# Convolution and maxout FFN on one core: who adds the two k1 halves, how PSUM tiles take turns, and where three buffers lie

## The chip, the cores and the metric

The kernel runs on one core of a Trainium2 chip. The metric is device time in microseconds, the median of several runs. TensorE (PE) multiplies matrices into PSUM; VectorE (DVE), ScalarE (ACT) and GpSimd (POOL) do the arithmetic around it; SyncE (SP), ACT and POOL issue the DMAs. In the rows of the profile PE is a matmul, PEld a weight load, and "q" behind an engine's name its sequencer or DMA queue. Line numbers are those of the kernel before; behind the diff's additions the same lines of the changed kernel stand one to some twenty further down.

## The reference

Four sequences of 12544 positions with 128 channels (`x`, `v`) go through a long convolution and then through a feed-forward block:

```python
h_filt = (np.maximum(pos_emb @ w1, 0) @ w2) * exp(-0.01 * pos)     # filter, 128 channels
u = x * v
y = irfft(rfft(u, 2S) * rfft(h_filt, 2S))[:S]                      # causal convolution along the sequence
x2 = (x * y).reshape(50176, 128)
h = np.maximum(np.maximum(x2 @ m1, x2 @ m2), x2 @ m3)              # 128 -> 768
out = h @ w_out                                                    # 768 -> 128
```

All is in float32. The kernel writes the maximum as `x2 @ m1` plus a maximum of relu and a difference: `max(relu(x2 @ (m2 - m1)), x2 @ (m3 - m1))`. The part with m1 goes through a product of m1 and w_out, `lin`, that is made once. So one hidden block of 128 costs two matmul groups, pa and pb, and one down projection.

## The kernel before, in words

**Stages.** A prologue (to about 320 us) converts weights, transforms the filter into the table hd in DRAM, and does the whole convolution of sequence 0 up to its last transform. Then come three passes of the main loop: the FFN of sequence b (0, 1, 2) runs on PE, and beside it, in small steps, the convolution of sequence b + 1. A last stage (from about 1913 us) does the FFN of sequence 3 with fewer products, sums of hidden blocks on POOL taking their place.

**The main loop.** Sequence b has 32 tiles (NT) of 4 x 98 positions, and each has six hidden blocks f (NF). One f of one tile is a slot; a pass has 192. In each slot `up` (L697) makes pa = 128x392 in PSUM (two halves of 64 columns, L154), relu into hid by ACT (L701), then pb, and DVE takes the maximum of hid and pb (L704). `down` (L710), two slots later, adds hid times w_out into ops; at the tile's end ACT copies ops to ot (L717) and POOL issues the store (L719).

**The last transform of the convolution.** For each tile, `t_load` fetches zt, two arrays z0 and z1 of 90x512 (two values of k1), and xT, through SP's queue. `t_sums` (L665) turns them into their sum (even, L669) and difference (zt, L670). In the later half of sequences 1 to 3 a sign is needed, and DVE does both with scalar_tensor_tensor (L673); elsewhere the engine is the caller's choice: POOL, and DVE for a sequence's first tile. They are called for the next tile at f = 0 (f = 3 in a sequence's last tile). `t_last` (L677) multiplies them by the table f4p into yps, at f = 3, 4 or 2, and DVE multiplies yps by xT into gt (L691), the FFN's input. The table f4p and a column of signs are loaded once, at the head of the main loop, through ACT's queue.

**The convolution beside it.** `conv_steps` (L575) plans it in slots. First the 32 units of the sequence are loaded, multiplied, transposed by DMA and put through the first transform (`u_first`, ps1, L408, DVE L419 into spec). When all are there, from slot s0 (55 for sequence 1, 62 for 2 and 3) on, 45 pairs g follow. A pair is: psq = middle transforms by matmul (`g_quarter`, L462 for pair g, L472 for the way back of pair z = g - 3), a fold (`g_fold`, ACT L484, DVE L487 twice into cb), swaps on ACT (`q_swap`), two multiplications by the filter ht on DVE (L506, L511), the add of the two on POOL (L514), and two unfolds on DVE (L518, cb to xs), which L472 needs three pairs on. POOL stores z to DRAM (`g_store`, L495).

The planner holds a table `load` of costs per slot. Folds have fixed slots; each multiplication and unfold is put into the emptiest slot of its allowed few. A slot in which DVE sums costs 1.4 more.

**Order.** [...] A matmul's bank is set when the program is built: a pool with n buffers gives out the one whose use ended first in the builder's order. The hps pool has three banks for pa and pb; cps has two double banks for ps1, psq and yps (three single ones in the last stage).

**Buffers.** hp holds zt, xT, even, gt and hid; op_ holds ot; op_ and the convolution's pools are released before the last stage, whose pool lp is laid over them. The last stage's relu results are in lp, and before its second block DVE makes five differences of parts of w_out and lin (L1090).

Of the kernel before, what the change touches and what calls it, by code (L numbers as in the profile page):

```python
# [1 line left out]

# [22 lines left out]
N1 = 90  # L25
NH = 82
HH = NH // 2
LATE = 3
# [61 lines left out]
def kernel(  # L90
# [15 lines left out]
    nc = tc.nc  # L106
    NG, _, _, B, NB = x.shape
# [3 lines left out]
    NF = DFF // P  # L111
    NK = N1 // 2
# [286 lines left out]
    def u_first(u, i0=0, n=4):  # L399


        t = uts[u] if i0 + n < 4 else uts.pop(u)
        ps = cps.tile([P, 256 * n], FP32, tag="cv", name="ps1")
        at = 4 * u + i0
        for i in range(n):
            for h in range(2):
                for c in range(2):
                    nc.tensor.matmul(  # L408
                        ps[64 * c:64 * c + 64, 256 * i + h * N1:256 * i + (h + 1) * N1],
                        t[:, 2 * ((at + i) % 8) + h].rearrange("n r t -> n (r t)"),  # L410
                        f1q[:, h, c * N1:(c + 1) * N1],
                        start=(i % 2 == 0 and h == 0), stop=True, skip_group_check=True)
        v = ps[:].rearrange("p (s m) -> p s m", m=256)[:, :, 0:2 * N1].rearrange(
            "p s (h k) -> p h k s", h=2)
# [37 lines left out]
    def g_quarter(g, z):  # L452


        ps = cps.tile([P, 1024], FP32, tag="cv", name="psq")
        if g is not None:
            w, t = ws.pop((g, 0)), sqs.pop(g)
            for k in range(2):
                for r in range(2):
                    for a in range(2):  # L460
                        at = 512 * r + k * D
                        nc.tensor.matmul(  # L462
                            ps[64 * a:64 * a + 64, at:at + D], w[64 * r:64 * r + 64, k, a, :],
                            t[64 * r:64 * r + 64, k, a, :], start=(k == 0), stop=True,
                            skip_group_check=True)
        if z is not None:
            w, ab = ws.pop((z, 1)), abs_.pop(z)
            for q in range(2):
                for a in range(2):
                    for k in range(2):  # L470
                        at = 512 * a + 256 + q * D
                        nc.tensor.matmul(  # L472
                            ps[64 * k:64 * k + 64, at:at + D], w[64 * a:64 * a + 64, k, q, :],
                            ab[64 * a:64 * a + 64, q, k, :], start=(g is None and q == 0),
                            stop=True, skip_group_check=True)
        pss[g, z] = ps
# [95 lines left out]
    def conv_steps(b, done):  # L572


        out = []  # L575
# [17 lines left out]
        def start(x):  # L593
            return s0 + int(x // 2 * 2 * per_pair)

        load = [(1.2 if i % NF == 3 else 0.6) + (1.4 if i % NF == 0 and b > 1 and i >= NT * NF // 2 else 0)
                for i in range(NT * NF)]
        for x in range(NK + LATE):
            s = start(x)
# [34 lines left out]
        return slots, {start(x) + 1 for x in range(NK + LATE)}  # L634


    N = 4 * NB
# [38 lines left out]

    def t_last(i):  # L677
        zt = zts.pop(i)
        ps = cps.tile([P, state["yps"]], FP32, tag="cv", name="yps")
        own = i[0] == B - 1 and i[1] > 1  # L680
        g = (lp if own else hp).tile([D, 4, NB], FP32, tag="g", name="gt", bufs=4 if own else 3)
        y = ps[:, 0:N].rearrange("d (p n) -> d p n", p=4)
# [12 lines left out]

    def up(i, f, tag="hid", bufs=3):
        rhs = gs[i][:].rearrange("d p n -> d (p n)")  # L697
        h = (lp if tag[0] == "h" and tag != "hid" else hp).tile([P, N], FP32, tag=tag, name="hid", bufs=bufs)
        pa = hps.tile([P, 512], FP32, tag="hps", name="pa")
        halves_mm(pa[:, 0:N], w_sb[1][:, f * P:(f + 1) * P], rhs, True, True)  # L700
        nc.scalar.activation(h[:], pa[:, 0:N], Relu)  # L701
        pb = hps.tile([P, 512], FP32, tag="hps", name="pb")
        halves_mm(pb[:, 0:N], w_sb[2][:, f * P:(f + 1) * P], rhs, True, True)
        nc.vector.tensor_tensor(out=h[:], in0=h[:], in1=pb[:, 0:N], op=ALU.max)  # L704
        return h
# [201 lines left out]
    state = {"cv": (cvp, cps), "turn": cps, "xb": 2}  # L907
    pl = sps.tile([D, 512], FP32, name="pl")
    Gs, minus = {}, {}

# [115 lines left out]
    hh = conv.enter_context(tc.tile_pool(name="hh", bufs=2))  # L1026
    cvp = conv.enter_context(tc.tile_pool(name="cvp", bufs=3))
    hps = ctx.enter_context(tc.tile_pool(name="hps", bufs=3, space=PSUM))
    cps = conv.enter_context(tc.tile_pool(name="cps", bufs=2, space=PSUM))
    ops = conv.enter_context(tc.tile_pool(name="ops", bufs=1, space=PSUM))  # L1030
    state = {"yps": 1024}


    tiles = [(b, i) for b in range(B) for i in range(NT)]
# [1 line left out]
    late = []  # L1036
    for n, (b, i) in enumerate(tiles[:LAST]):
        if i == 0:
            beside, folds = conv_steps(b + 1, EARLY if b == 0 else 0)
        if n == 0:  # L1040
            t_load(*tiles[0])
            t_load(*tiles[1])
# [2 lines left out]
        for f in range(NF):  # L1045
# [29 lines left out]


    lp = ctx.enter_context(tc.tile_pool(name="lp", bufs=1))
    cps = ctx.enter_context(tc.tile_pool(name="cps2", bufs=3, space=PSUM))
    state["yps"] = 512
# [83 lines left out]
```

## Time and profile before

| | |
|---|---|
| median of 3 runs | 2338.91 us (2336.47 to 2343.64) |
| profiled execution | 2339.31 us, span 2337.5 us |
| mean granted PE clock | 0.996 |
| busy: PE, DVE, ACT, POOL | 2284.1, 1553.8, 1178.8, 969.0 us |
| L704 DVE maximum | 768, mean 558 ns |
| L701 ACT relu | 768, mean 499 ns |
| L518 DVE unfold | 270, mean 662 ns |
| L514 POOL add | 135, mean 1306 ns |
| L669, L670 on POOL | 61 each, mean 1304 and 1302 ns |
| L669, L670 on DVE | 19 each, mean 1041 and 942 ns |
| L673 on DVE, even and zt | 48 each, mean 870 and 972 ns |
| zt from issue to landing (384 issues of 90 KB) | median 3.1 us |

The profile is of one execution. A row of a timeline gives start, duration, engine, line, operation and tiles; in brackets is the engine's idle time before it and what ended it. A row "x3" is three instructions merged, with the time from the first start to the last end. A row of waits gives who waited for whom: total us, times, longest. Means of a group hide that one instruction can take much longer than another of the same shape. The end of a matmul is modelled: neighbouring matmuls overlap in the rows, so start-to-start is the time that one takes; a group of four pa matmuls starts 0.66 us after the one before it.

### The profile page before, as it was taken

How to read it: one execution, taken by the hardware profiler on the slowest of the kernel's cores; microseconds unless marked ns; L12 is line 12 of the kernel's file. 1: busy time of each engine (PE TensorE's matmuls, PEld its weight loads, DVE VectorE, ACT ScalarE, POOL GpSimd, SP SyncE). 2: the span in 40 equal slices, each digit the busy share in tenths (PEclk: the TensorE clock that was granted, in tenths of full speed). 3: DMA queues.
4: the chain of work that ended last, by engine and by line, in shares of the span. 5: the costliest groups of instructions: out<-in, count | busy, mean ns of one | idle time of the engine just before them, and what ended most of it. 6: DMA issues, size and time to landing. Idle time of an engine off the chain costs nothing.

```text
span 2337.5 us, 68165 instructions
## 1 busy us (share of the span) xinstructions
PE 2284.1 (98%) x27853; PEld 1371.9 (59%) x27853; DVE 1553.8 (66%) x2798; ACT 1178.8 (50%) x2124; POOL 969.0 (41%) x1153
## 2 busy tenths in 40 slices
PE   8999989999999999999999999999999999999998
PEld 7889856655455445655555546655555546666665
DVE  5678856656777746757888846757888855454443
ACT  2678844456666624446666634446666622222222
POOL 1045424424444424324333324324333326666666
PEclk9999999999999999999999999999999999999999
DMA  7868969989998749979999849969999822222221
GB/s 160 201 202 266 290 158 181 165 180 238 226 238 219 198 104 187 188 141 238 240 248 246 226 113 180 192 144 244 242 241 245 223 80 66 54 54 70 65 55 22
DMA packets 473146, 410.93 MB, mean 176 GB/s; under 512 B 328004, under 2 KB 374231, under 8 KB 472834
## 3 DMA queue, kind: packets, MB, share of 16 engines
q1 hardware_dynamic: 433504, 317.61, 62.2%
q0 software_dynamic: 26400, 75.72, 11.2%
q10 hardware_dynamic: 12930, 13.25, 1.8%
q8 instruction: 219, 3.59, 0.7%
q14 instruction: 93, 0.76, 0.1%
HBM read 262.77 MB, written 84.67 MB: 149 GB/s over the span
## 4 chain that ended last, share of the span: by engine, by line
PE 76%; DMA 11%; DVE 5%; issue 3%; ACT 2%; SPq 1%; POOL 0%; ACTq 0%; DVEq 0%; POOLq 0%
PE pa L154 18%; PE pb L154 17%; PE ops L154 14%; PE ops L764 6%; PE ps L408 5%; DMA ht<-hd 4%; PE yps L154 4%; PE ps L163 3%; PE ps L154 2%; DMA zt<-zd 2%; PE psq L472 2%; DVE xs L518 2%; PE psq L462 2%; DMA sq<-spec 2%; DMA wt<-wq_const 1%
## 5 line engine op out<-in xcount | busy, mean ns | idle before, releaser
L701 ACT ACTIVATE hid<-pa 128x392 f32<-128x392 f32 x768 | 383.5, 499 | 756.5 <-PE pa L154 738.3
L704 DVE TENSOR_TENSOR hid<-hid,pb 128x392 f32<-128x392 f32 x768 | 428.2, 558 | 361.9 <-PE pb L154 351.5
L154 PE MATMUL pb<-gt,w_sb 128*64 128x392 f32 x3072 | 640.3, 495 | 10.2 <-ACT hid L701 10.2
L154 PE MATMUL pa<-gt,w_sb 128*64 128x392 f32 x3072 | 644.8, 497 | 0.7 <-DVE gt L691 0.7
L154 PE MATMUL ops<-hid,wo_sb 128*64 128x392 f32 x2304 | 478.1, 493 | 0.0
L154 PEld LDWEIGHTS pb<-gt,w_sb 128*64 128x64 f32 x3072 | 220.6, 137 | 301.2 <-issue 263.2
L514 POOL TENSOR_TENSOR cb<-cb,xs 128x512 f32<-128x512 f32 x135 | 176.3, 1306 | 455.1 <-DVE xs L511 210.5
L154 PEld LDWEIGHTS ops<-hid,wo_sb 128*64 128x64 f32 x2304 | 167.0, 137 | 212.9 <-issue 212.9
L154 PEld LDWEIGHTS pa<-gt,w_sb 128*64 128x64 f32 x3072 | 200.6, 137 | 147.6 <-issue 124.4
L419 DVE TENSOR_TENSOR spec<-ps,high 128x360 f32<-128x360 f32 (+1 forms) x204 | 142.1, 739 | 131.2 <-ACT high L417 130.8
L487 DVE TENSOR_TENSOR cb<-psq,eo 128x512 f32<-128x512 f32 (+1 forms) x288 | 175.3, 650 | 75.1 <-ACT eo L484 74.6
L719 POOL DMA_DIRECT2D out_dram<-ot x96 | 75.3, 785 | 322.2 <-ACT ot L717 293.7
L502 ACT ACTIVATE xs<-cb 32x512 f32<-32x512 f32 x270 | 169.9, 629 | 22.2 <-DVE cb L487 13.4
L518 DVE TENSOR_TENSOR xs<-cb 128x256 f32<-128x256 f32 x270 | 167.5, 662 | 9.8 <-POOL cb L514 9.8
L503 ACT COPY xs<-cb 32x512 f32<-32x512 f32 x270 | 166.7, 617 | 3.2
L417 ACT COPY high<-ps 128x360 f32<-128x360 f32 (+1 forms) x102 | 77.2, 761 | 157.2 <-PE ps L408 126.3
L408 PEld LDWEIGHTS ps<-f1q,uT 98*64 98x64 f32 x3072 | 131.8, 137 | 35.2 <-issue 32.9
L154 PEld LDWEIGHTS yps<-f4p,even 90*64 90x64 f32 x2048 | 116.1, 139 | 40.9 <-issue 35.0
L408 PE MATMUL ps<-f1q,uT 98*64 98x90 f32 x3072 | 136.4, 241 | 3.2 <-DVE spec L419 2.6
L691 DVE TENSOR_TENSOR gt<-yps,xT 128x392 f32<-128x392 f32 x128 | 72.3, 565 | 91.7 <-PE yps L154 52.6
L154 PE MATMUL yps<-f4p,even 90*64 90x49 f32 x2048 | 125.7, 221 | 3.0 <-DMA f4p<-f4p_const 3.0
L154 PE MATMUL yps<-f4p,zt 90*64 90x49 f32 x2048 | 127.3, 223 | 0.0
(130 smaller groups left out, 3306.7 us busy)
## 6 DMA issues: line engine op xcount, KB each, us to landing
ht<-hd SPq DMA_DIRECT2D x264, 256.0 KB, 6.7
wt<-wq_const SPq DMA_DIRECT2D x144, 256.0 KB, 6.4
zd<-cb POOLq DMA_DIRECT2D x135, 256.0 KB, 6.2
zt<-zd SPq DMA_DIRECT2D x384, 90.0 KB, 3.1
sq<-spec SPq DMA_DIRECT2D x264, 128.0 KB, 7.0
ut<-in_xr_dram SPq DMA_DIRECT2D x128, 196.0 KB, 4.3
ut<-in_vr_dram SPq DMA_DIRECT2D x128, 196.0 KB, 4.6
xT<-in_x_dram SPq DMA_DIRECT2D x256, 98.0 KB, 3.6
```

The lines of the kernel that those rows point to most:

```text
L154: nc.tensor.matmul(out[64 * h:64 * h + 64], lhsT[:, 64 * h:64 * h + 64], rhs, start=start, stop=stop, skip_group_check=True)
L408: nc.tensor.matmul(ps[64 * c:64 * c + 64, 256 * i + h * N1:256 * i + (h + 1) * N1], t[:, 2 * ((at + i) % 8) + h].rearrange("n r t -> n (r ...
L417: nc.scalar.copy(high, v[:, 0])
L419: nc.vector.tensor_tensor(out=spec[:, :, a, at:at + n], in0=v[:, 1], in1=high, op=op)
L487: nc.vector.tensor_tensor(out=cb[:, a, lo:hi], in0=ps[:, lo:hi], in1=eo[:, lo:hi], op=op)
L502: nc.scalar.mul(xs[at:at + 32], xt[at + 32:at + 64], -1.0)
L503: nc.scalar.copy(xs[at + 32:at + 64], xt[at:at + 32])
L514: nc.gpsimd.tensor_tensor(out=xts[g], in0=xts[g], in1=xs[:], op=ALU.add)
L518: nc.vector.tensor_tensor(out=ab[:, q], in0=y[:, 0], in1=y[:, 1], op=(ALU.subtract, ALU.add)[q])
L701: nc.scalar.activation(h[:], pa[:, 0:N], Relu)
L704: nc.vector.tensor_tensor(out=h[:], in0=h[:], in1=pb[:, 0:N], op=ALU.max)
L764: nc.tensor.matmul(ps[64 * c:64 * c + 64, 0:H2], w, rhs[:, H2 * c:H2 * c + H2], start=start, stop=True, skip_group_check=True)
```

## The change

1. `t_sums` goes to DVE also for tiles whose slot lies past s0, while pairs run: the sums of tiles 11 to 31 of sequence 0 and of tiles 12 to 15 of sequences 1 and 2. `conv_steps` returns s0 (`pairs_from`), and its `load` counts 1.4 for f = 0 of every tile past s0, not just of the later half.
2. PSUM tiles are made once and taken in turns by `itertools.cycle`: three banks for pa and pb, two double banks for ps1, psq and yps, three single ones for yps in the last stage. In the prologue the pool stays.
3. hid has a pool of its own (hidp), which stays in the last stage; its first three relu results use it. op_ lies with the pools that stay. The five differences are made one at a time after steps 3 to 7 of the last stage instead of all at its start.
4. f4p and the signs are loaded through SP's queue, ahead of the first zt.

```diff
-        ps = cps.tile([P, 256 * n], FP32, tag="cv", name="ps1")
+        ps = state["bank"]()[:, 0:256 * n]
...
-        ps = cps.tile([P, 1024], FP32, tag="cv", name="psq")
+        ps = state["bank"]()
...
-        load = [(1.2 if i % NF == 3 else 0.6) + (1.4 if i % NF == 0 and b > 1 and i >= NT * NF // 2 else 0)
+        load = [(1.2 if i % NF == 3 else 0.6) + (1.4 if i % NF == 0 and i > s0 else 0)
...
-        ps = cps.tile([P, state["yps"]], FP32, tag="cv", name="yps")
+        ps = state["bank"]()
...
-        h = (lp if tag[0] == "h" and tag != "hid" else hp).tile([P, N], FP32, tag=tag, name="hid", bufs=bufs)
-        pa = hps.tile([P, 512], FP32, tag="hps", name="pa")
+        h = (hidp if tag == "hid" else lp).tile([P, N], FP32, tag=tag, name="hid", bufs=bufs)
+        pa = next(hbanks)
...
-        pb = hps.tile([P, 512], FP32, tag="hps", name="pb")
+        pb = next(hbanks)
...
+    hidp = ctx.enter_context(tc.tile_pool(name="hidp", bufs=3))
     hp = ctx.enter_context(tc.tile_pool(name="hp", bufs=3))
+    f4p = hp.tile([N1, 2, 2, NB // 2], FP32, name="f4p", bufs=1)
+    nc.sync.dma_start(f4p[:], f4p_d)
+    sign_t = hp.tile([N1, 1], FP32, name="sign", bufs=1)
+    nc.sync.dma_start(sign_t[:], sign_d)
+    op_ = ctx.enter_context(tc.tile_pool(name="op", bufs=2))
     conv = ExitStack()
-    f4p = hp.tile([N1, 2, 2, NB // 2], FP32, name="f4p", bufs=1)
-    nc.scalar.dma_start(f4p[:], f4p_d)
-    sign_t = hp.tile([N1, 1], FP32, name="sign", bufs=1)
-    nc.scalar.dma_start(sign_t[:], sign_d)
...
-    op_ = conv.enter_context(tc.tile_pool(name="op", bufs=2))
...
+    hbanks = itertools.cycle([hps.tile([P, 512], FP32, name=f"hps{i}") for i in range(3)])
+    pairs = itertools.cycle([cps.tile([P, 1024], FP32, name=f"cps{i}") for i in range(2)])
+    state = {"bank": lambda: next(pairs)}
...
-                t_sums(tiles[n + 1], nc.vector if turn_ else nc.gpsimd)
+                t_sums(tiles[n + 1], nc.vector if turn_ or i * NF > pairs_from else nc.gpsimd)
...
-    for out, a, b in ((tw[:, 1], b22, b12), (b12, b12, b11), (tw[:, 0], b22, b12),
-                      (tw[:, 2], b21, tw[:, 0]), (linx[:], lin[:, 0:64], lin[:, 64:128])):
-        nc.vector.tensor_tensor(out=out, in0=a, in1=b, op=ALU.subtract)
+    weights = [(tw[:, 1], b22, b12), (b12, b12, b11), (tw[:, 0], b22, b12),
+               (tw[:, 2], b21, tw[:, 0]), (linx[:], lin[:, 0:64], lin[:, 64:128])]
...
+            own = (name, BUFS[name]) if step > 2 else ("hid", 3)
             h[name, f] = first if step == 0 else up(
-                (b, i + n), f + (NC if name[2] == "2" else 0), name, BUFS[name])
+                (b, i + n), f + (NC if name[2] == "2" else 0), *own)
+            if step > 2 and weights:
+                out, a1, a2 = weights.pop(0)
+                nc.vector.tensor_tensor(out=out, in0=a1, in1=a2, op=ALU.subtract)
```

More of the change, by code (lines that the diff above doesn't have):

```diff
@@ L1 @@
+import itertools
 from contextlib import ExitStack
@@ L412, in u_first @@
                         start=(i % 2 == 0 and h == 0), stop=True, skip_group_check=True)
-        v = ps[:].rearrange("p (s m) -> p s m", m=256)[:, :, 0:2 * N1].rearrange(
+        v = ps.rearrange("p (s m) -> p s m", m=256)[:, :, 0:2 * N1].rearrange(
             "p s (h k) -> p h k s", h=2)
@@ L633, in conv_steps @@
             slots.setdefault(s, []).append((fn, args))
-        return slots, {start(x) + 1 for x in range(NK + LATE)}
+        return slots, {start(x) + 1 for x in range(NK + LATE)}, s0
     N = 4 * NB
@@ L906 @@
     sps = pro.enter_context(tc.tile_pool(name="sps", bufs=1, space=PSUM))
-    state = {"cv": (cvp, cps), "turn": cps, "xb": 2}
+    state = {"cv": (cvp, cps), "turn": cps, "xb": 2,
+             "bank": lambda: cps.tile([P, 512], FP32, tag="cv", name="ps1")}
     pl = sps.tile([D, 512], FP32, name="pl")
@@ L1027 @@
     cvp = conv.enter_context(tc.tile_pool(name="cvp", bufs=3))
-    hps = ctx.enter_context(tc.tile_pool(name="hps", bufs=3, space=PSUM))
-    cps = conv.enter_context(tc.tile_pool(name="cps", bufs=2, space=PSUM))
+    hps = ctx.enter_context(tc.tile_pool(name="hps", bufs=1, space=PSUM))
+    cps = conv.enter_context(tc.tile_pool(name="cps", bufs=1, space=PSUM))
     ops = conv.enter_context(tc.tile_pool(name="ops", bufs=1, space=PSUM))
-    state = {"yps": 1024}
+    hbanks = itertools.cycle([hps.tile([P, 512], FP32, name=f"hps{i}") for i in range(3)])
+    pairs = itertools.cycle([cps.tile([P, 1024], FP32, name=f"cps{i}") for i in range(2)])
+    state = {"bank": lambda: next(pairs)}
     tiles = [(b, i) for b in range(B) for i in range(NT)]
@@ L1038 @@
         if i == 0:
-            beside, folds = conv_steps(b + 1, EARLY if b == 0 else 0)
+            beside, folds, pairs_from = conv_steps(b + 1, EARLY if b == 0 else 0)
         if n == 0:
@@ L1077 @@
     lp = ctx.enter_context(tc.tile_pool(name="lp", bufs=1))
-    cps = ctx.enter_context(tc.tile_pool(name="cps2", bufs=3, space=PSUM))
-    state["yps"] = 512
+    cps = ctx.enter_context(tc.tile_pool(name="cps2", bufs=1, space=PSUM))
+    singles = itertools.cycle([cps.tile([P, 512], FP32, name=f"last{i}") for i in range(3)])
+    state = {"bank": lambda: next(singles)}
     ops = ctx.enter_context(tc.tile_pool(name="ops2", bufs=1, space=PSUM))
```

## The prediction

> **What bounds the kernel now.** I read the busy shares first, then what TensorE (PE) waits for, then those waits in the timeline.
>
> ```profile
> span 2337.5 us, 68165 instructions
> PE 2284.1 (98%) x27853; PEld 1371.9 (59%) x27853; DVE 1553.8 (66%) x2798; ACT 1178.8 (50%) x2124; POOL 969.0 (41%) x1153
> ```
>
> PE is busy for 2284.1 of 2337.5 us, and the change alters no matmul: the built programs have the same PE order. All it can move is the 53.4 us in which PE stands, and what follows from it. The waits of PE (total, times, longest) over the whole run:
>
> ```profile
> PE pb L154 <- ACT hid L701: 10.2, 12, 3.5
> PE psq L472 <- DVE xs L518: 9.6, 15, 1.0
> PE yps L154 <- DMA f4p<-f4p_const: 3.0, 1, 3.0
> PE psq L472 <- DVE gt L691: 3.0, 1, 3.0
> ```
>
> Nearly all others lie in the opening, which the change leaves alone. The same view for 500 to 830 us alone, where the pairs of sequence 1 run beside the FFN of sequence 0:
>
> ```profile
> PE psq L472 <- DVE xs L518: 4.4, 5, 1.0
> PE psq L472 <- DVE gt L691: 3.0, 1, 3.0
> PE pb L154 <- ACT hid L701: 3.0, 4, 0.9
> ```
>
> Three mechanisms stand behind these rows. **(a)** The PSUM pools give out whichever bank was free first in the build's order. Of 768 pb tiles ten are put where the pa of the same step lies, so PE must wait for that pa's relu. The gaps before pb number exactly ten of 0.59 to 0.91 us, 6.6 us in all (10.2 less the 3.5 of (c) and one of 0.2): 3.0 in this stretch, 3.6 at the starts of sequences 0, 1 and 2. **(b)** psq waits for late L518 results. The timeline shows why (start, us, engine, line):
>
> ```profile
> 630.39 1.27 POOL L514 TENSOR_TENSOR cb<-cb,xs 128x512 f32<-128x512 f32 x1 [5.32 <-ACT hid L701]
> 630.64 4.66 DVE L518 TENSOR_TENSOR xs<-cb 128x256 f32<-128x256 f32 x3
> 632.23 1.37 POOL L669 TENSOR_TENSOR even<-zt 90x512 f32<-90x512 f32 x1
> 633.67 1.34 POOL L670 TENSOR_TENSOR zt<-zt 90x512 f32<-90x512 f32 x1
> ...
> 635.35 0.45 PE L472 MATMUL psq<-xs,wt 64*64 64x128 f32 x8 [0.96 <-DVE xs L518]
> ```
>
> An L518 alone has a median of 419 ns; these three took 4.66 us. One lasted for the add L514 on POOL, one for both sums, L669 and L670. Then psq stands for 0.96 us. Set against POOL's spans, 16 of the 90 L518 here overlap a POOL sum and hold 19.1 us above 419 ns. At 818.19 the same triple (4.64 us) delays gt and gives the 3.0 us wait. **(c)** At the change to the last stage a relu writes memory that output buffers still occupy:
>
> ```profile
> 1912.70 0.76 POOL L719 DMA_DIRECT2D out_dram<-ot  x1 [11.30 <-ACT ot L717]
> 1916.70 0.89 ACT L701 ACTIVATE hid<-pa 128x392 f32<-128x392 f32 x2 [4.31 <-DMA out_dram<-ot]
> 1917.25 1.57 PE L154 MATMUL pb<-gt,w_sb 128*64 128x392 f32 x4 [3.46 <-ACT hid L701]
> 1918.62 1.52 PE L154 MATMUL pa<-gt,w_sb 128*64 128x392 f32 x4
> 1920.93 0.82 PE L154 MATMUL pa<-gt,w_sb 128*64 128x392 f32 x4
> ```
>
> PE stands 3.46 us before pb at 1917.25. After it four pb matmuls last 1.57, and only at 1920.93 0.82 again: three groups take 3.68 us for 1.98, 1.70 us more. After the 3.05 us wait at 820.8 four groups take 4.38 for 2.63, 1.75 more.
>
> [...] 33 L518 beside L514 and the store's issue have a median of 1316 ns for 419, while L704, with one input in PSUM, stays at 557 beside L514. [...]
>
> **The change part by part**, against the profiled execution's 2339.3 us (1.8 of it outside the span; 0.4 above the median of the three).
>
> 1. Strict turns. Every bank is now reused by the third tile on, so the ten waits go: -6.6. But 136 pa tiles used the bank two back, and 136 pb tiles four back; all become three. I set each tile's start in the trace against the end of the reader three tiles earlier: the room is negative only at six pa tiles (1118, 1199, 1295, 1644, 1725, 1821 us), by 0.67 each, because the L704 before is late. That costs 4.0. Within some 5 us after each there is a psq wait of 0.22 to 0.42, 2.1 together, and a PE that starts later finds that L518 done: +1.9 net. For psq and yps the same comparison at two turns gives nothing negative. ACT gets 218 extra semaphore waits before relu; a satisfied one takes 17 ns, and the room of pb behind relu is mostly 1.26 us: 0.
>
> 2. Sums on DVE. 21 tiles of sequence 0 and 4 each of sequences 1 and 2, two instructions each: 58 x 0.68 us (L669 at 325.53, row below). In 500 to 830 DVE gains 42 x 0.68 = 28.7 and loses the 19.1. A moved sum can itself be blocked by L514: in the second halves of sequences 1 and 2, where DVE already sums, 12 of 32 tiles had one that was, by some 0.9; the same share here is 8 of 21, 7 us. So 241.7 becomes some 258 of 330, 78%. Two stretches already run in that state:
>
> ```profile
> 500.00:830.00 330.00, 319.33 (x3572) 164.75 (x3570) 241.69 (x410) 200.51 (x362) 155.62 (x151) 0.99 0.89 218
> 1210.00:1370.00 160.00, 159.55 (x1754) 81.45 (x1750) 126.61 (x223) 96.56 (x176) 50.90 (x54) 1.00 0.85 212
> 1700.00:1872.00 172.00, 171.08 (x1948) 88.48 (x1946) 143.05 (x248) 110.60 (x199) 59.89 (x62) 1.00 0.96 234
> ```
>
> There DVE is at 79% and 83%, and PE stands for 0.45 of 160 and 0.92 of 172 us. That is the best evidence that DVE bears it. Queued behind a sum on DVE are the first L704 of the tile and the pair's arithmetic; for L704 waits pa two steps on. Its room there is mostly 1.78 us, and 0.78 in four tiles (from 565, 582, 696, 713 us): 1.37 - 0.78 = 0.6 x 4 = 2.4. At 820 L518 is blocked by L514 alone, 2.0 shorter: 1.05 remains, too little for the half clock. I leave 0.5 for the first pair. This stretch now loses 10.4 + 1.75 = 12.2 and will lose 4.0: -8.2, of which 3.0 is counted in 1: -5.2. In sequences 1 and 2 the waits of 0.95 at 1068 and 1593, beside POOL sums, go: -1.9. Zt lands 9 us or more before DVE would want it, so no DMA is waited for. The planner moves eight unfolds and two multiplications of the conv of sequence 1, and one unfold each of sequences 2 and 3, by one slot, within the limits that psq's need sets: 0.
>
> 3. Relu buffers, output buffers, table differences. The relu no longer waits for the output's landing: -3.46 - 1.70 = -5.2. The five subtractions (1.7 us) go between L704s; DVE is half idle there (159 of 330 us), and they are needed from step 9: 0.
>
> 4. f4p and sign through SP. Two issues (0.63 and 0.34 us on ACT) stand ahead of zt and xT in SP's queue. f4p no longer lands last, but zt does:
>
> ```profile
> 325.53 0.69 DVE L669 TENSOR_TENSOR even<-zt 90x512 f32<-90x512 f32 x1 [0.30 <-DMA zt<-zd]
> ```
>
> About 1.0 later, the sums end at 327.2 and 327.9, where yps started at 327.11 before. From -0.3 to +1.5; I take +0.6.
>
> Sum: -6.6 + 1.9 - 5.2 - 1.9 - 5.2 + 0.6 = -16.4. 2339.3 - 16.4 = 2322.9; against the median 2338.9, some 2323.
>
> **Rivals.** A: DVE's queue loosens more than I allow, no pa waits, and all psq waits go: 6.6 + 9.6 + 3.05 + 1.75 + 5.2 = 26 saved, 2313. For it: PE's 99.7% at 79% DVE. Against it: the six negative rooms. B: lateness moves from psq to pa, and the stretch keeps its 12.2; sequences 1 and 2 gain nothing. Only 3.6 + 5.2 - 0.6 is won: 2331. For it: strict turns take from pb the four-back room that the build gave just where DVE is late. C, slower: DVE becomes the bound. If L514 blocked a sum in every one of the 29 moved tiles for its whole 1.3 us, the first L704 would come 2.67 later against room 1.78: 0.89 x 25 + 1.89 x 4 = 29.8, less the 2.4 counted: 2350. It decides once the moved tiles lose over 0.8 us each (16.4 + 7 over 29). Against it: 12 of 32. That the change doesn't do what it says is excluded for the order: the build has the 58 sums on DVE and all turns at three and two.
>
> **How the numbers follow.** Mine 0.62, A 0.14, B 0.18, C 0.06. Unknown costs (f4p 2 us, blocked sums some 4, pa waits 2 to 4) spread mine from 2318 to 2330. The range 2315 to 2332 leaves out much of A, part of B and C. This kernel's runs differ by 0.3%, 7 us, and less can't be told from no change; 2331.9 is the border. Faster: nearly all of mine, A, half of B: 0.83; same 0.11; slower 0.06.
>
> **What would show it.** Right: no wait of pb for relu above 0.3 us; no clock dip near 820 and 1915; L518 beside L669 gone; PE standing some 4 us in 500 to 830; pa waiting for DVE hid, about ten times, 0.6 each. Wrong: pa waits for L704 in most moved tiles (C, or B if psq's remain), sums at 1.5 us or more on the mean, or yps waiting past 328 for zt.

## The result, and the profile after

The changed kernel takes 2316.97 us (median of four runs, 2315.53 to 2319.48). The kernel before takes 2339.88 (median of four). The ratio is 0.9903, with a 95% interval of 0.9885 to 0.9921: faster by 1%, some 23 us. The forecast was 2323, with a range of 2315 to 2332.

The busy shares of the changed kernel (columns as before):

```profile
span 2313.7 us, 68365 instructions
PE 2277.5 (98%) x27853; PEld 1379.8 (60%) x27853; DVE 1574.2 (68%) x2856; ACT 1177.5 (51%) x2124; POOL 898.8 (39%) x1095
```

PE is busy for 2277.5 us, not 2284.1, although not one matmul was changed, and it stands for 36.2 us, not 53.4. Of the gain of 23.8 us between the two profiled spans, 17.2 is idle time and 6.6 is "busy" time. The prediction had treated busy time as fixed but for the two stretches at the half clock. This is where it fell short, as shown below.

The waits of PE over the whole run, in the changed kernel. Its PSUM tiles have new names: hps is pa or pb, cps is ps1, psq or yps. Columns are total us, times, longest.

```profile
PE hps L155 <- DVE hid L705: 5.3, 10, 0.9
PE cps L155 <- DVE even L670: 2.8, 1, 2.8
PE cps L473 <- DVE gt L692: 0.5, 1, 0.5
```

The ten pb waits for relu, the fifteen psq waits for xs, the 3.0 us for gt and the 3.5 us at the change to the last stage are gone. In their place stand ten waits of hps (pa) for L705 (the old L704), as the prediction said, and one of 0.5 for gt. The 2.8 us for the first sum takes the place of the 3.0 us for f4p. The same view for 500 to 830 us:

```profile
PE hps L155 <- DVE hid L705: 1.7, 4, 0.4
PE cps L473 <- DVE gt L692: 0.5, 1, 0.5
```

The prediction gave these places 2.4 and 1.05. The load on VectorE there, and in two stretches where it already made the sums before, comes from the view of windows (us, then busy time and instructions of PE, PEld, DVE, ACT, POOL; clock; DMA share; GB/s):

```profile
500.00:830.00 330.00, 327.77 (x3664) 169.60 (x3662) 262.60 (x458) 202.26 (x366) 105.62 (x111) 1.00 0.89 221
1190.00:1350.00 160.00, 159.43 (x1778) 82.08 (x1776) 128.16 (x226) 98.17 (x179) 53.01 (x56) 1.00 0.84 213
1678.00:1850.00 172.00, 170.83 (x1976) 89.16 (x1974) 143.02 (x250) 111.68 (x201) 59.01 (x61) 1.00 0.97 239
```

DVE is busy for 262.6 of 330 us (forecast: some 258), POOL for 105.6 instead of 155.6, and PE stands for 2.2 us instead of 10.7. The triple of L518 that took 4.66 us beside POOL's sums is now L519, and the sums, now on DVE, run after it instead of beside it (timeline of the changed kernel: start, us, engine, line):

```profile
626.83 1.26 POOL L515 TENSOR_TENSOR cb<-cb,xs 128x512 f32<-128x512 f32 x1 [5.42 <-DVE xs L512]
626.97 2.07 DVE L519 TENSOR_TENSOR xs<-cb 128x256 f32<-128x256 f32 x3
628.97 0.68 DVE L670 TENSOR_TENSOR even<-zt 90x512 f32<-90x512 f32 x1
629.12 0.62 PE L473 MATMUL cps<-xs,wt 64*64 64x128 f32 x16
629.68 0.69 DVE L671 TENSOR_TENSOR zt<-zt 90x512 f32<-90x512 f32 x1
```

The triple takes 2.07 us, one of its three still being long beside L515; the sums follow at 0.68 and 0.69, and L473 starts without a wait. At the change to the last stage (timeline):

```profile
1893.48 0.76 POOL L720 DMA_DIRECT2D out_dram<-ot  x1 [11.31 <-DMA zt<-zd]
1894.62 0.50 ACT L702 ACTIVATE hid<-hps 128x392 f32<-128x392 f32 x1 [0.82 <-DVE hid L705]
1892.76 6.42 PE L155 MATMUL hps<-gt,w_sb 128*64 128x392 f32 x38
```

The store is issued at the same point of the work, but the relu after it, which used to wait 4.31 us for its landing, waits for a maximum only, and PE runs through without a gap.

To see where the time comes from I cut the profiled executions at the ends of the maxima (L704, L705 in the changed kernel), counted from one. The column "before" is the length of a stretch in the kernel before; all other numbers are differences to it, in us.

| stretch, by count of L704 | before | forecast | changed | turns alone | sums alone | buffers alone |
|---|---|---|---|---|---|---|
| start to 1 | 333.36 | +0.6 | +0.59 | +0.49 | +2.23 | +0.17 |
| 1 to 60, no pairs | 167.38 | -1.2 | -1.66 | -1.42 | +0.28 | +0.05 |
| 60 to 186, pairs of sequence 1 | 343.03 | -8.2 | -11.18 | -4.24 | -10.84 | -0.02 |
| 192 to 258, no pairs | 190.50 | -1.2 | -1.65 | -1.63 | 0.00 | -0.02 |
| 258 to 384, pairs of sequence 2 | 334.93 | 0 | -1.74 | +0.38 | -1.58 | +1.01 |
| 385 to 571, all of sequence 3 beside the FFN | 512.19 | -1.2 | -3.59 | -0.96 | -0.78 | -0.17 |
| 571 to 591, change to the last stage | 45.43 | -5.2 | -4.54 | +0.29 | -0.47 | -4.54 |
| 591 to the end | 395.26 | 0 | -0.01 | 0.00 | 0.00 | -0.01 |

The stretches left out differ by less than 0.02. Three rows carry noise of up to some 2 us: the start, because the prologue ends at 324.1 us in one execution and at 326.2 in another, and the two rows with the first pairs of sequences 2 and 3, where PE waits by turns for L518 or for a DMA (wt, sq), 0 to 1.5 us in all. The last three columns are the experiments that follow.

### The profile page after: what moved, and what is told of

Same layout as the page of the kernel before. It is cut to its first block, busy times and chain, and to the rows that moved or that the text cites. A ratio compares the mean times of both kernels' runs of the same rounds, so it can differ in the third digit from the quotient of the medians.

```text
span 2313.7 us, 68365 instructions
## 1 busy us (share of the span) xinstructions
PE 2277.5 (98%) x27853; PEld 1379.8 (60%) x27853; DVE 1574.2 (68%) x2856; ACT 1177.5 (51%) x2124; POOL 898.8 (39%) x1095
## 3 DMA queue, kind: packets, MB, share of 16 engines
q0 software_dynamic: 26400, 75.72, 11.2%
q8 instruction: 219, 3.59, 0.7%
## 4 chain that ended last, share of the span: by engine, by line
PE 84%; DMA 6%; ACT 3%; DVE 3%; issue 2%; SPq 1%; ACTq 1%; POOL 0%; DVEq 0%; POOLq 0%
PE hps L155 41%; PE ops L155 17%; PE ops L765 6%; PE cps L409 5%; PE cps L155 4%; PE cps L463 3%; PE ps L164 3%; PE cps L473 2%; DMA ht<-hd 2%; PE last L155 1%; DMA hd<-ht 1%; ACT ht L958 1%; DMA wt<-wq_const 1%; PE pm L324 1%; DMA zt<-zd 1%
## 5 line engine op out<-in xcount | busy, mean ns | idle before, releaser
L155 PE MATMUL hps<-gt,w_sb 128*64 128x392 f32 x6144 | 1150.4, 495 | 6.1 <-DVE hid L705 5.3
L702 ACT ACTIVATE hid<-hps 128x392 f32<-128x392 f32 x768 | 383.9, 500 | 736.6 <-PE hps L155 720.7
L155 PEld LDWEIGHTS hps<-gt,w_sb 128*64 128x64 f32 x6144 | 424.5, 137 | 437.4 <-issue 391.3
L705 DVE TENSOR_TENSOR hid<-hid,hps 128x392 f32<-128x392 f32 x768 | 427.3, 557 | 333.6 <-PE hps L155 323.9
L515 POOL TENSOR_TENSOR cb<-cb,xs 128x512 f32<-128x512 f32 x135 | 181.7, 1346 | 471.4 <-DVE xs L512 331.1
L488 DVE TENSOR_TENSOR cb<-cps,eo 128x512 f32<-128x512 f32 (+1 forms) x288 | 175.1, 649 | 65.6 <-ACT eo L485 65.1
L420 DVE TENSOR_TENSOR spec<-cps,high 128x360 f32<-128x360 f32 x180 | 135.5, 794 | 121.9 <-ACT high L418 121.9
L519 DVE TENSOR_TENSOR xs<-cb 128x256 f32<-128x256 f32 x270 | 141.8, 568 | 7.5 <-POOL cb L515 7.5
L409 PEld LDWEIGHTS cps<-f1q,uT 98*64 98x64 f32 x2880 | 124.9, 137 | 30.6 <-issue 30.6
L409 PE MATMUL cps<-f1q,uT 98*64 98x90 f32 x2880 | 128.1, 241 | 0.4 <-DVE uT L393 0.4
L155 PE MATMUL cps<-f4p,even 90*64 90x49 f32 x1568 | 96.5, 221 | 2.8 <-DVE even L670 2.8
L155 PE MATMUL cps<-f4p,zt 90*64 90x49 f32 x1568 | 97.8, 223 | 0.3 <-DVE zt L671 0.3
```

Of the source, the lines that this page charges most:

```text
L155: nc.tensor.matmul(out[64 * h:64 * h + 64], lhsT[:, 64 * h:64 * h + 64], rhs, start=start, stop=stop, skip_group_check=True)
L409: nc.tensor.matmul(ps[64 * c:64 * c + 64, 256 * i + h * N1:256 * i + (h + 1) * N1], t[:, 2 * ((at + i) % 8) + h].rearrange("n r t -> n (r ...
L488: nc.vector.tensor_tensor(out=cb[:, a, lo:hi], in0=ps[:, lo:hi], in1=eo[:, lo:hi], op=op)
L515: nc.gpsimd.tensor_tensor(out=xts[g], in0=xts[g], in1=xs[:], op=ALU.add)
L519: nc.vector.tensor_tensor(out=ab[:, q], in0=y[:, 0], in1=y[:, 1], op=(ALU.subtract, ALU.add)[q])
```

## The experiments

### The parts one by one

**Strict turns alone.** The kernel before with

```diff
-        pa = hps.tile([P, 512], FP32, tag="hps", name="pa")
+        pa = next(hbanks)
...
-        ps = cps.tile([P, 1024], FP32, tag="cv", name="psq")
+        ps = state["bank"]()
```

(and the same for pb, ps1 and yps). Expected:

> The kernel before with the strict turns alone (part 1); sums, relu and output buffers and the load of f4p as before. My theory: the ten waits of pb for the relu of its own step go (6.6 us in the rows, and some 0.17 more for each, 1.7, because a matmul behind a wait shows no overlap with the one before it), and some six waits of pa for the late L704 of about 0.67 appear near 1118, 1199, 1295, 1644, 1725 and 1821 us, which take the place of six psq waits of 0.22 to 0.42: -4.7 to -6 us against the kernel before. The psq waits of 0.8 to 1.0 between 500 and 830 us, the one of 3.0 at 821 with the clock dip, and the wait of 3.46 at 1917 all stay. Rival B: with turns of three, DVE's lateness in the tiles with sums on POOL is passed on to pa; then the stretch from 500 to 830 us loses as much as before and only the waits at the starts go: -3.6 us or less.

Measured: 2332.67 beside 2340.52, ratio 0.9965 (0.9952 to 0.9977): 7.9 us shorter, more than the 4.7 to 6 expected. In the stretch of the table's third row the four waits, 3.0 us in the rows, are worth 3.9 by start times; most of the rest of the 4.24 lies at the half clock near 820 us. Its waits of PE from 500 to 830 us:

```profile
PE cps L473 <- DVE xs L519: 4.4, 5, 1.0
PE cps L473 <- DVE gt L692: 3.0, 1, 3.0
```

The four pb waits are gone and everything else in the stretch stays, the 3.0 us at gt too. No pa wait takes their place here, so rival B falls: while POOL makes the sums, L704 is never late enough for pa. In sequences 2 and 3, where DVE already made the sums, six pa waits of 0.54 to 0.55 appear where the prediction had set them (1111, 1192, 1289, 1636, 1717 and 1814 us in this run).

**Sums on DVE alone**, with the planner's costs.

```diff
-                t_sums(tiles[n + 1], nc.vector if turn_ else nc.gpsimd)
+                t_sums(tiles[n + 1], nc.vector if turn_ or i * NF > pairs_from else nc.gpsimd)
...
-        load = [... + (1.4 if i % NF == 0 and b > 1 and i >= NT * NF // 2 else 0)
+        load = [... + (1.4 if i % NF == 0 and i > s0 else 0)
```

> The kernel before with the sums on DVE wherever pairs run, and the planner's costs with it (part 2), alone. My theory: L518 instructions that last over 2.5 us between 500 and 830 us vanish, and with them the psq waits there (4.4 and 3.0 us in the rows, the clock dip near 825), and the waits of 0.95 at 1068 and 1593 us: -7.1 us by the prediction, -9 to -10 if all psq waits there go and each brings 0.17 more. The ten waits of pb for relu stay (6.6 us), also those between 500 and 830. DVE is busy some 258 to 263 of the 330 us there. Rival C: DVE becomes the bound, L704 comes late and pa or pb waits for it in most moved tiles: no gain, or slower.

Measured: 2326.88, ratio 0.9943 (0.9930 to 0.9955): 13.6 us shorter. This part is the largest. Waits of PE from 500 to 830 us:

```profile
PE pb L154 <- ACT hid L701: 1.2, 2, 0.6
PE psq L472 <- DVE xs L518: 0.8, 2, 0.4
PE psq L472 <- DVE gt L691: 0.5, 1, 0.5
```

The psq waits for xs fall from 4.4 to 0.8 us, that for gt from 3.0 to 0.5, and the half clock near 825 is gone (granted clock 1.00 from 824 to 829). Rival C falls: DVE is at 263.4 of 330 us and PE still stands for 2.5. Two of the four pb waits, those of 0.9, are gone as well, which I had not expected; presumably because the pool deals out banks in the order of the build and the moved sums change that order, but the trace doesn't tell banks. So turns and sums overlap: -4.24 and -10.84 make -15.1 alone, and -11.18 together. From this kernel to the changed one, by start times, the two pb waits left (0.82 us each) go, two pa waits (0.64 each) come, and two more take the place of the psq waits of 0.4: once the sums have moved, strict turns are worth 0.34 us in this stretch. There is no pa wait for L704 here, though two sums stand in a row on DVE: those waits need the turns as well.

**Buffers alone** (hidp, op_ among the pools that stay, the five differences apart).

```diff
-        h = (lp if tag[0] == "h" and tag != "hid" else hp).tile([P, N], FP32, tag=tag, name="hid", bufs=bufs)
+        h = (hidp if tag == "hid" else lp).tile([P, N], FP32, tag=tag, name="hid", bufs=bufs)
...
-    op_ = conv.enter_context(tc.tile_pool(name="op", bufs=2))
+    op_ = ctx.enter_context(tc.tile_pool(name="op", bufs=2))
```

> The kernel before with part 3 alone: a pool of its own for hid that stays in the last stage, the output buffers among the pools that stay, the five differences one at a time. My theory: the wait of 3.46 us of pb at 1917 and the half clock after it go, -4.5 to -5.2 us, all at the change to the last stage; everything before 1910 us is unchanged within 0.3 us. Rival: the store's landing is not the cause; the wait stays or goes to the five differences, and the time is the same.

Measured: 2335.74, ratio 0.9979 (0.9971 to 0.9987): 4.8 us shorter, and in the trace -4.54 at the change to the last stage. It is not the whole 5.2: two waits of yps for zt, the difference that DVE makes, 0.40 and 0.40, come to light there that the long wait had covered.

**f4p back on ACT's queue**, in the changed kernel.

```diff
-    nc.sync.dma_start(f4p[:], f4p_d)
+    nc.scalar.dma_start(f4p[:], f4p_d)
```

> The changed kernel with part 4 undone: f4p and the signs are loaded through the queue of ScalarE again. My theory: the first yps waits for f4p and starts at about 327.1 us as in the kernel before; the sums on DVE end before it, and the time is 0 to 0.6 us shorter than the changed kernel's. Rival: f4p on the queue of ScalarE was what delayed the first yps in the kernel before, and undoing part 4 costs time: 1 us or more longer than the changed kernel's.

Measured: 2318.35, ratio to the kernel before 0.9904 (0.9891 to 0.9918), the changed kernel's own within its interval. The traces tell more than the medians. From the end of PE's last matmul of the prologue to the end of the first maximum it takes 9.37 us here and 9.30 to 9.66 (mean 9.44) in all five kernels with f4p on ACT; in the seven with f4p on SP, those below included that leave this gap as it is, it takes 9.57 to 9.83 (mean 9.69). The first yps waits 3.15 us for f4p here, 2.82 and 0.26 for the sums in the changed kernel. On ACT's queue f4p lands 2.9 to 3.3 us after that last matmul, just behind the end of the sums (2.5 to 2.9). On SP's queue it is issued ahead of the first zt (320.83 and 321.80 us) and has landed 1.6 us or more before the prologue ends, but the second zt lands some 0.9 us later, and the sums end at 3.5 to 3.7. So part 4 gains nothing; it costs about a quarter of a microsecond.

### Why sums on GpSimd cost time

GpSimd's sums could do harm in two ways: by blocking VectorE, or by delaying what stands behind them in GpSimd's own queue, the add L515 and the stores. In the 29 moved tiles of the changed kernel I put two extra instructions on GpSimd, in one kernel additions that read SBUF, in the other memsets that read nothing. Nobody reads their results.

```diff
+                    for _ in range(2):
+                        z0 = zts[tiles[n + 1]][0]
+                        nc.gpsimd.tensor_tensor(out=junk[:, 0:512], in0=z0, in1=z0, op=ALU.add)
```

> The changed kernel with two extra additions on GpSimd in each of the 29 tiles whose sums moved (z0 + z0 into a scratch tile that nobody reads; the output is unchanged). They have the place, the shape and, at 1.3 us, the length of the sums that GpSimd made before. Theory of the blocked VectorE: L519 (and a sum) beside them takes over a microsecond more, 12 to 20 us in all between 500 and 830 us, psq waits of 0.8 to 1.0 and the long one near 815 come back, and the kernel is 5 to 9 us longer than the changed one. Rival, GpSimd's queue: what mattered in the kernel before was that the add L515 and the stores stood behind the sums; then L519 starts late, but does not last longer, and the time is lost in the same places.

```diff
+                    for _ in range(2):
+                        nc.gpsimd.memset(junk[:].bitcast(U16), 0)
```

> The changed kernel with two extra memsets of a scratch tile (90x1408 of 16 bit, estimated at 1.3 us each from the 308 ns of the planes' 128x240 memset and the 0.1 us of a memset of one element) in the same places: GpSimd is as busy as with the additions, but reads nothing. Theory of the blocked VectorE: L519 beside a memset stays near 419 ns, and the time is the changed kernel's within 1 us. Rival, GpSimd's queue: the same loss as with the additions, 5 to 9 us.

Measured: 2331.44 with additions, ratio 0.9958 (0.9943 to 0.9973), and 2316.60 with memsets, 0.9899 (0.9882 to 0.9915). The additions cost some 14 us, more than expected; the memsets cost nothing. Waits of PE from 500 to 830 us with the additions:

```profile
PE cps L473 <- DVE xs L519: 4.5, 7, 0.7
PE cps L473 <- DVE gt L692: 2.5, 1, 2.5
PE hps L155 <- DVE hid L705: 1.7, 4, 0.4
```

and with the memsets:

```profile
PE hps L155 <- DVE hid L705: 1.7, 4, 0.4
PE cps L473 <- DVE gt L692: 0.4, 1, 0.4
```

The same triple in the timeline, with additions:

```profile
631.74 4.19 DVE L519 TENSOR_TENSOR xs<-cb 128x256 f32<-128x256 f32 x3
633.33 2.31 POOL L1066 TENSOR_TENSOR junk<-zt 90x512 f32<-90x512 f32 x2
635.98 0.45 PE L473 MATMUL cps<-xs,wt 64*64 64x128 f32 x8 [0.73 <-DVE xs L519]
```

and with memsets, which last 1279 ns each on the mean, longer than the additions' 1225:

```profile
627.27 1.98 DVE L519 TENSOR_TENSOR xs<-cb 128x256 f32<-128x256 f32 x3
628.83 2.70 POOL L1065 MEMSET junk<- 90x1408 uint16 x2
629.41 0.62 PE L473 MATMUL cps<-xs,wt 64*64 64x128 f32 x16
```

POOL is busy for 155.5 and 158.2 of the 330 us, so its queue is equally full. But an L519 that runs beside an extra addition and no other instruction of GpSimd has a median of 1043 ns (15 in the whole run), one beside a memset 410 ns (14); alone it has 419. The queue theory falls: L519, whose inputs both lie in SBUF, is stretched beside the addition, which reads SBUF, and not beside the memset, which only writes it. The loss is larger than expected, probably because nothing was taken from DVE for it: the sums are there and the blocks come on top (273.3 us busy). The long wait at gt comes back (2.5 us) with its half clock (0.66 on the mean from 824 to 829 us).

### What is left

DVE's ten late L705 could come from L515, which still blocks L519 and the sums (23.4 us between 500 and 815 us in the changed kernel), or from two sums in a row ahead of one L705. The first is tried with the add on DVE:

```diff
-        nc.gpsimd.tensor_tensor(out=xts[g], in0=xts[g], in1=xs[:], op=ALU.add)
+        nc.vector.tensor_tensor(out=xts[g], in0=xts[g], in1=xs[:], op=ALU.add)
```

> The changed kernel with the pair's add (L515, 135 times, 1.3 us on GpSimd) on VectorE, some 0.75 us each. Theory of the blocked VectorE: VectorE gains 45 x 0.75 = 34 us between 500 and 830 us and loses the 23 us by which L515 stretches its own L519 and sums there; it is busy some 273 of 330 us, the pa waits of 0.42 to 0.54 shrink or go, and the time is 0 to 5 us shorter than the changed kernel's. Rival: at 83% VectorE is the bound; L705 comes late in more tiles and the time is 3 us or more longer.

and the second with the sums a slot apart:

```diff
+            if f == 1 and own_sums:
+                t_sums(tiles[n + 1], nc.vector, (1,))
...
-(1.4 if i % NF == 0 and i > s0 else 0)
+(0.7 if i % NF < 2 and i > s0 else 0)
```

> The changed kernel with the two sums of a tile a slot apart wherever pairs run (even at f = 0, the difference at f = 1; the planner counts 0.7 for each). If the pa waits come from two sums in a row ahead of one L705, as the prediction's step 2 has it, then one sum (0.68, or some 1.5 blocked) fits the room of 0.8 to 1.8 us: the ten or so pa waits (5.3 us in the rows, some 0.2 more for each) go, and the time is 4 to 7 us shorter than the changed kernel's. Rival: VectorE's lateness there comes from the pair's own arithmetic, and splitting only moves the waits: within 2 us.

Measured: 2310.55, ratio 0.9871 (0.9857 to 0.9886), with the add on DVE; 2309.91, 0.9870 (0.9855 to 0.9885), with the sums apart. The changed kernel is 22.9 us under the kernel before, these two are 30.2 and 30.9 under the runs of it beside them: some 7 to 8 us shorter. Windows of 500 to 830 us, first with the add on DVE, then with the sums apart:

```profile
500.00:830.00 330.00, 328.34 (x3676) 170.78 (x3676) 268.85 (x501) 202.11 (x366) 46.97 (x66) 1.00 0.89 220
```

```profile
500.00:830.00 330.00, 328.45 (x3676) 170.96 (x3674) 250.50 (x460) 203.48 (x369) 106.74 (x111) 1.00 0.90 222
```

The add brings DVE 43 more instructions in this window and only 6.3 us more time: no L519 and no sum there is stretched any more (the longest take 0.42 and 0.69 us). Yet the ten pa waits stay, at 0.36 and 0.48 instead of 0.42 and 0.54, so the blocking was not their main cause. The gain comes in small steps: PE's waits after the first maximum fall only from 7.5 to 6.6 us in all, but by start times its groups come 0.05 to 0.4 us earlier at dozens of places. Most of these delays are shorter than the 0.17 us by which neighbouring rows overlap, and so they stood in no row. With the sums apart the pa waits are all gone. Its sums are not stretched by L515 either (none of 42 takes over 0.69 us, while ten took 1.65 in the changed kernel), but the run with the add on DVE shows that this alone leaves the waits. So their cause is two sums in a row ahead of one L705, together with the strict turns (the planner's half of this edit has little weight, to judge by the last run of this section). What comes next in line is small: eight waits of 0.37 of psq for gt, and 0.81 at the last of them instead of 0.47.

Both together:

> The changed kernel with both: the pair's add on VectorE, and the two sums a slot apart. My theory: each alone won 6 to 7 us, but partly the same waits; VectorE is busy some 269 us of the 330 between 500 and 830 us, its instructions are not stretched there, no pa waits remain and of the eight waits of 0.37 for gt most go: 8 to 11 us shorter than the changed kernel, 2306 to 2309. Rival: with all of it on VectorE the gains don't add, and L705 comes late again: not shorter than the split alone (2310).

Measured: 2310.62, ratio 0.9868 (0.9854 to 0.9883). The gains don't add in the time, though they do in the stretch: PE is busy for 329.2 of 330 us there. The profiled execution shows its next limit at other places, waits of 0.87 and 0.49 for the table wt, which comes by DMA through SP's queue. The prologue of that execution also ended late, at 326.4 us. Which of these holds the gain back can't be settled from one execution and stays open.

The planner's costs put back to those of the kernel before, in the changed kernel (its `load` line):

> The changed kernel with the planner's costs as before (1.4 for f = 0 only in the later halves of sequences 2 and 3): eight unfolds and two multiplications of sequence 1's pairs stand a slot earlier or later than in the changed kernel. Prediction's step 2: this is worth 0; within 1 us of the changed kernel. Rival: the planner's move is what keeps the unfolds off the slots with sums; without it psq waits or longer pa waits come between 500 and 830 us, 2 us or more in all.

Measured: 2317.34, ratio 0.9900 (0.9884 to 0.9917), no difference in the time. Two psq waits of 0.2 come up at 600 and 728 us, 0.5 us in the stretch. The prediction's zero for the planner is right to within that.

### The gap at the start of the main loop

The largest wait that remains is that of the first yps, and the granted clock is 0.50 for 6.8 us from there. The changed kernel with matmuls in the gap:

```diff
             t_sums(tiles[0], nc.vector)
+            spare = [next(hbanks) for _ in range(3)][2]
+            for _ in range(4):
+                halves_mm(spare[:, 0:N], w_sb[1][:, 0:P], w_sb[2][:, 0:N], True, True)
```

> The changed kernel with four extra groups of matmuls (w_sb times w_sb, 2.6 us at the full clock, into a PSUM bank that is not yet in use; results are not read) in the gap of 2.8 to 3.0 us ahead of the first yps. Theory, from the clock records: the gap makes the clock fall to half from 326.6 to 333.4 us, and three pa and pb groups that should take 0.66 us each start 1.33, 1.30 and 1.14 apart; with the gap filled the dip goes, and the first hid comes 1.8 to 2.5 us earlier after the end of the prologue. Rival: the clock falls for another reason (the end of a phase), the dip stays, and the time is the same or 0.3 us longer.

Measured: 2315.56, ratio 0.9888 (0.9874 to 0.9903). The time alone doesn't tell it from the changed kernel. The trace does (PE, timeline):

```profile
327.04 2.85 PE L155 MATMUL hps<-w_sb,w_sb 128*64 128x392 f32 x16 [1.32 <-DVE spec L420]
329.70 0.30 PE L155 MATMUL cps<-f4p,even 90*64 90x49 f32 x4
...
331.47 4.17 PE L155 MATMUL hps<-gt,w_sb 128*64 128x392 f32 x24 [0.66 <-DVE gt L692]
```

The granted clock is 1.00 from 322 to 336 us. The six groups of pa and pb take 4.17 us, where the changed kernel's first five took 5.00. From the last matmul of the prologue to the first maximum it is 7.98 us instead of 9.59: 1.6 shorter. It is less than it could be. The first extra matmul waits 1.32 us for an instruction of the prologue on DVE (L420), so the extra work ends at some 329.9 while the first sum is ready at 328.6; two groups might have been enough, which wasn't tried.

All three together:

> The changed kernel with the add on VectorE, the split sums and the extra matmuls in the first gap: the gains of the two runs before it in this set should add, as they lie in different stages: 10 to 13 us shorter than the changed kernel, 2304 to 2307.

Measured: 2307.11, ratio 0.9857 (0.9843 to 0.9872): 33.7 us less than the kernel before and some 11 less than the changed one, the shortest of this study. Its profiled execution was its longest, 2312.2, and shows waits that the changed kernel has in part only (waits of PE, 1560 to 1905 us):

```profile
PE cps L463 <- DMA wt<-wq_const: 1.8, 4, 0.7
PE cps L463 <- DMA sq<-spec: 0.3, 1, 0.3
```

In the changed kernel it is one wait of 0.34 for wt in that stretch. A likely reading is that PE, having lost its waits for DVE, comes earlier to the tables that SP's queue brings; no run here tests it, and such waits differ between executions.

## Why the prediction was right, and where it fell short

The mechanism held, and the time, 2317.0, lies 6 us under the forecast, 2 us inside the range. It was not luck in the sense of errors that cancel: nearly all of them lie on the same side, and the gain is almost half as large again as forecast. Step by step, by the trace (-16.4 forecast, -23.8 measured):

**Step 1, ten waits of pb at 6.6 us.** They go, but they are worth more than their rows. This is the term that was mis-sized, and it is the same in step 2. The kernel before, PE, where one such wait stands:

```profile
569.23 0.83 PE L154 MATMUL pa<-gt,w_sb 128*64 128x392 f32 x4
569.89 0.83 PE L154 MATMUL pb<-gt,w_sb 128*64 128x392 f32 x4
...
571.86 0.83 PE L154 MATMUL pa<-gt,w_sb 128*64 128x392 f32 x4
573.59 0.88 PE L154 MATMUL pb<-gt,w_sb 128*64 128x392 f32 x4 [0.90 <-ACT hid L701]
```

A group starts 0.66 us after the one before it, but its row lasts 0.83, because rows of neighbouring matmuls overlap by 0.17. Behind a wait there is nothing to overlap. pb starts 1.73 us after pa, 1.07 late, while the row of the wait says 0.90; and the row behind the wait is 0.05 longer (0.88). So a wait costs some 0.22 us more than it shows. In stretches 1 to 60 and 192 to 258, which hold two such waits of 0.6 each and little else, the gain is 1.66 and 1.65, 0.83 for each. After the first maximum PE has 41 gaps of 24.0 us in the kernel before and 23 gaps of 7.5 in the changed one, and its busy time falls from 1972.7 to 1965.0. 18 gaps fewer by 0.22 is 4.0 us, and with the 3.45 us of the two stretches at half clock this is nearly the whole of these 7.7 us. Up to the first maximum the changed kernel is busy 1.1 us longer, with one more stretch at half clock (at 313 us), which leaves the 6.6.

**Step 1, six pa waits of 0.67, +1.9 net.** The waits are right, the net isn't. The rows show five of 0.54 and one of 0.89; with 0.17 more each the five are 0.71. But the psq waits whose place they take, 0.22 to 0.42 in the rows, are worth up to 0.64 by start times, so that four of the six cost next to nothing and all six together some 0.8. The room had been taken from start times, which hold the overlap, while what was removed had been summed from rows, which don't. Mixing the two made the gain too small.

**Step 2, the stretch from 500 to 830 us: 12.2 lost before, 4.0 left, -8.2.** Measured -11.18. By start times, what went is worth 14.0 us instead of 11.2: the five waits for xs 5.8 (4.4 in the rows), the four of pb 3.9 (3.0), the wait at gt 2.6 of its 3.05 (2.0 forecast), the half clock 1.7. What came is worth 2.8 of the 2.9 forecast. The four pa waits came as predicted, at the four tiles named (567, 583, 695 and 711 us), 0.42 in the row and 0.59 in time, 0.64 with the row behind it, for the 0.6 forecast. The first of them in the timeline of the changed kernel:

```profile
565.66 0.68 DVE L670 TENSOR_TENSOR even<-zt 90x512 f32<-90x512 f32 x1
566.37 0.69 DVE L671 TENSOR_TENSOR zt<-zt 90x512 f32<-90x512 f32 x1
566.98 1.02 DVE L705 TENSOR_TENSOR hid<-hid,hps 128x392 f32<-128x392 f32 x2
...
567.59 1.54 PE L155 MATMUL hps<-gt,w_sb 128*64 128x392 f32 x8 [0.42 <-DVE hid L705]
```

Two sums and two L705 in a row on DVE, and PE waits for the second. The wait at gt is 0.47 instead of 1.05, and the 0.5 left for the first pair isn't there. Blocked sums were 10 of 21 tiles (forecast 8), 9.6 us (forecast 7); DVE carried it.

**Steps 1 and 2 in sequences 2 and 3: 0 and -1.2.** Measured -1.74 and -3.59. By start times the two waits of 0.95 beside POOL's sums are worth 1.5 each, the two of pb 0.82 each, and the six pa waits cost the 0.8 said above. Two psq waits of 0.55 and 0.64 at the first pairs (1054 and 1579 us in the kernel before), which the prediction left out, are gone too. What that is worth, 0.9 and 0.5 in these executions, mixes with the waits for DMAs there and is not settled.

**Step 3, -5.2.** Measured -4.54: right, less the two zt waits behind it (0.31 and 0.40), for which the step should have asked what is late next.

**Step 4, +0.6.** The +0.59 in the table agrees by chance: 0.30 of it is the prologue, which ended later in that execution. The sums ended at 327.1 and 327.9 us, as forecast, but over five and seven kernels the step costs 0.25, since f4p was nearly as late before.

**The rivals.** A gave 2313 for no pa wait and no psq wait. Half of it came true: the psq waits all went, but the pa waits stayed, and the changed kernel lies between A and the forecast, nearer to A. B had the stretch lose as much as before; it is 11.18 us shorter. C had DVE as the bound; with the sums alone the stretch is 10.84 us shorter.

## What to carry to other kernels

A wait of TensorE is worth its row plus the overlap that its neighbours would have had, here some 0.22 us; take both what goes and what comes from start times, or both from rows. Parts of a change can overlap: strict turns were worth 4.24 us in one stretch alone and 0.34 on top of the moved sums. When a sum is moved between GpSimd and VectorE, look first at what runs beside it on the other engine and what it reads; here L519 had a median of 1043 ns beside an addition on GpSimd and of 410 beside a memset. Two instructions ahead of one that is waited for may stand a slot apart; here that was worth 8 us, as much as moving the add to VectorE.

## What the runs showed of the hardware

Up to PE's last matmul, the granted clock was 0.50 in every dip of the kernel before and of the changed one, and each lasted 3.41 us, or 6.83 at the start of the main loop. From 150 us on, the dips of the kernel before start at 326.58, 824.93 and 1917.20 us, which is 146 and 320 times 3.413 us apart; those of the changed kernel start at 312.96 and 326.61 us, 4 times. I laid off stretches of that length from these starts and took PE's busy share in each by its rows. The stretch ahead of a dip had 0.25, 0.32 and 0.00 in the kernel before (waits of 3.05, 3.05 and 3.46 us), 0.48 and 0.30 in the changed one (1.77 and 2.82). Of the stretches at full clock that no dip followed, the emptiest had 0.57 (from 265.1 and 265.2 us). Inside the two long dips the clock stayed at half after stretches of 0.63 and 0.64. What happens between 0.48 and 0.57 these two traces don't show.

One wait came out both ways. PE waits 1.77 us for spec near the end of the prologue in both kernels. In the changed kernel the wait runs from 311.14 to 312.91 us, within one of these stretches, and the dip at 312.96 follows. In the kernel before it runs from 312.28 to 314.05, over the border of two at 312.93; PE is busy for 0.81 and 0.61 of them, and no dip follows. In the kernel with the extra additions PE stands for 2.53 us between 820 and 824 us, and the mean clock from 824 to 829 is 0.66. Shorter waits at full clock were followed by no dip in the two traces from 150 us on, among them 1.47 at 266.8 and at 266.4 us, and 1.07 at 289.1. So the prediction's "too little for the half clock", its author's estimate for a wait of 1.05, agrees with the kernel before.

A memset on GpSimd of 1.28 us left the L519 beside it at a median of 410 ns, where an addition on GpSimd of 1.22 us brought L519 to 1043; alone L519 has 419.
